# Halves of the pair's last unit two slots sooner and ahead of exponentials; the last eight sums of w_in one a step

## The chip, the cores and the metric

The kernel runs on one core of one Trainium2 chip. The metric is the device time of one execution in microseconds; the median of three runs is given. The core has TensorE (PE, matrix products), VectorE (DVE) and ScalarE (ACT) for elementwise work, GpSimd (POOL) and SyncE (SP), which here do hardly more than issue DMAs, and DMA engines that all queues share.

## The reference

Attention within chunks of 64 tokens, then an MLP with a leaky activation, then a bilinear MLP. All is float32; 2304 tokens, 512 features.

```python
# q, k, v: (4, 8, 576, 64); chunk 64
scores = scale * np.matmul(q_c, k_c.transpose(0, 1, 2, 4, 3))
attn = np.exp(scores - np.max(scores, axis=-1, keepdims=True))
attn = attn / (np.sum(attn, axis=-1, keepdims=True) + 1e-09)
out = np.matmul(attn, v_c)
x = out.transpose(0, 2, 1, 3).reshape(2304, 512)   # after the chunks are joined
h = x @ w_in                                       # 512 x 2048
x = (np.maximum(h, 0.0) + alpha * np.minimum(h, 0.0)) @ w_out
return (x @ w_a) * (x @ w_b) @ w2_out              # 512 x 1536, 1536 x 512
```

## The kernel before

Tokens are cut into 18 units of 128 (u = 0 to 17) and five blocks of 512, 256, 512, 512 and 512 tokens, so that units 10 to 17 make up the last two blocks, which the kernel calls the pair. Float32 operands are split into a high and a low half, and a product is three matmuls (`three`, L396): the names end in h and l. The weights of the first MLP lie in SBUF as such halves (`wi0h`, `wi0l` and so on).

The third block is the stretch of the change, some 184 to 291 us of the profile. It runs the first MLP of units 6 to 9 in 16 steps j. A step multiplies x by w_in (`psh`, 12 matmuls), `prelu` takes it through ACT (`neg` L414, `pos` L415), DVE (`pos` L416), ACT (`gh` L87) and DVE (`gl` L92), and one step later the result is multiplied by w_out into the accumulators (`acc`, 12 matmuls). Each step has two slots, 2j ahead of `prelu` and 2j+1 behind the matmuls of w_out (`advance`). Into these slots `att_line` puts the attention of the pair, by a table `at` of slots, one number for each unit. Steps are sorted by slot, and within a slot they stand in the order in which the list was put together. Engines run their instructions in program order, so this order is the order on every engine and queue.

For a unit of the pair the steps are these:

- `load_kq` (L245, issued by POOL): k and q into a buffer `kq`.
- `apart` (calls `halves`, L262 and L264): ACT copies k, then q, into the two 16-bit halves of each number (`kqd`, 128x1024 each), SP stores them to DRAM as `rowsk` and `rowsq`.
- `turn_qk` (calls `turned`, L269), two slots after `apart`: SP issues two DMA transposes that bring them back as `kT` and `qT`.
- `att_S` (L315) in `multiply`: 32 small products into `psSO`. Called S12 and so on here. In the same step the output product of the unit three before is made (`att_O`, L372), called O14 and so on. Its result goes through ACT (`xh`, or `x` for the last block) and DVE.
- `att_M` (DVE, L328 and L330), `soften` (exponential on ACT, L336, then the normalization on DVE, L341 to L345).
- the turn of e: by PE (`att_PT`) for units 10 to 13, by `halves` and a DMA transpose (`ed`, `rowse`, `eT`) for 14 to 17.

Unit 15's k and q are turned by PE instead (`att_kq`, `psT`, L298, with ACT copies `kT`, `qT`, L300). The PSUM pool of `psh`, `psSO`, `psT` and `psP` has four banks which go round.

The first eight sums of w_in (high half plus low half, DVE, L159) and their stores to DRAM (`wd`, POOL, L160) are made in an earlier block; the last eight in steps 8 to 11 of this one, two a step (`keep_w`). They are read back (`wir`) for the preparation of the second MLP. From slot 23 on, `y_sums` (L1248) and `begin_t` put DVE work for the second MLP into the same stretch; the last of these, `Txl` (L92), is needed by the first products of the second MLP (`psE`, L1348).

Of the kernel before, what the change touches and what calls it, by code (L numbers as in the profile page):

```python
# [18 lines left out]
def chunk_attention_prelu_mlp_bilinear_mlp(  # L19
# [17 lines left out]
    nc = tc.nc  # L37
# [9 lines left out]
    J1 = F1 // P  # L47
# [28 lines left out]
    def bank(nm="ps"):  # L76
        return ps_p.tile([P, DM], F32, tag="ps", name=nm)
# [5 lines left out]
    def wtile(name, dt=F32R):  # L83
        return wp.tile([P, DM], dt, tag="w", name=name)
# [67 lines left out]
    wparts = {}  # L152
    wd = [dr.tile([P, DM], F32, name=f"wd{j}") for j in range(J1)]

    def keep_w(j):

        hi, lo = W["i", j]
        x = wtile("wi", F32)
        nc.vector.tensor_tensor(out=x, in0=hi.bitcast(F32), in1=lo.bitcast(F32), op=ALU.add)  # L159
        nc.gpsimd.dma_start(out=wd[j], in_=x)  # L160

    def unpack_parts(i):
        u = unpack_ops(i, True)
# [86 lines left out]
    def load_v(u, queue=None):  # L250
        load("v", u, queue)
# [55 lines left out]
    def att_S(u, pss=None):  # L307
        qT, kT = att.pop(("qT", u)), att.pop(("kT", u))
        pss = pss or [att_bank(u, "psS") for _ in range(2)]
        for y in range(2):  # L310
            for c in range(2):
                for e in range(2):
                    for x in (e, 1 - e):
                        i = half(e), 2 * x + y, c
                        nc.tensor.matmul(  # L315
                            out=pss[e][half(x), half(2 * y + c)], lhsT=qT(*i), rhs=kT(*i),
                            start=True, stop=True,
                        )
        att["s", u] = pss
# [45 lines left out]
    def att_O(u, xh, xl, col, pss=None):  # L365
        eT, v_ = att.pop(("eT", u)), att.pop(("v", u))
        pss = pss or [att_bank(u, "psO") for _ in range(2)]
        for g in range(KD):
            x, y = divmod(g, 2)
            for c in range(2):  # L370
                for e in (c, 1 - c):
                    nc.tensor.matmul(  # L372
                        out=pss[c][half(e), half(g)], lhsT=v_[half(c), half(2 * g + e)],
                        rhs=eT[half(c), half(4 * e + 2 * y + x)], start=True, stop=True,
                    )
        cols = [slice(col + c * CH, col + (c + 1) * CH) for c in range(2)]
        return [
            (xh[:, :, f], None if xl is None else xl[:, :, f], ps[:, :KD * CH].rearrange("p (g i) -> p g i", g=KD))
            for f, ps in zip(cols, pss)
        ]  # L380
# [688 lines left out]
    def att_line(bx, x, ut, sums_of):  # L1069

        t0, n = blocks[bx]
        us = range(t0 // P, NU)
        LAG = 3

        def dest(u):
            if u * P < t0 + n:
                return *x, u * P - t0
            ut[u] = wtile(f"x{u}", F32).rearrange("p (k t) -> p k t", k=KD)
            return ut[u], None, 0

        def out_of(u, pss):
            o = att_O(u, *dest(u), pss)
            if u + 2 < NU:
                load_v(u + 2, nc.gpsimd)
            return o

        def multiply(w):
            pss = [bank("psSO") for _ in range(2)]
            now, then_ = us[w:w + 1], us[max(w - LAG, 0):max(w - LAG + 1, 0)]
            for u in now:  # L1090
                att_S(u, [ps[:, :KD * CH] for ps in pss])
            o = sum((out_of(u, [ps[:, KD * CH:] for ps in pss]) for u in then_), [])
            each(to_hi, o)

            def after():
                for u in now:
                    att_M(u)
                each(to_lo, o)

            return after  # L1100

        def soften(u):
            att_X(u)
            return lambda: weave(att_N(u))

        def out_only(*ws):
            pss = [bank("psSO") for _ in range(2)]
            o = sum((out_of(us[w], [ps[:, i * KD * CH:(i + 1) * KD * CH] for ps in pss])
                     for i, w in enumerate(ws)), [])
            each(to_hi, o)  # L1110
            return lambda: each(to_lo, o)

        def only(fn, *a):
            def step():
                fn(*a)
                return lambda: None

            return step

        at = {  # L1120
            "S": (0, 3, 6, 10, 13, 16, 19, 22), "turn": (5, 8, 11, 14), "out": (17, 19, 21, 25),
            "apart": (None, None, 1, 5, 7, None, 13, 17), "load": (None, None, None, 1, 4, 7, 10, 13),
        }
        steps = [(slot, lambda w=w: multiply(w)) for w, slot in enumerate(at["S"])]
        steps += [(slot + 1, lambda u=u: soften(u)) for u, slot in zip(us, at["S"])]
        steps += [(slot, only(att_PT, u, True)) for u, slot in zip(us, at["turn"])]
        steps += [(slot + 2, only(att_PT_in, u)) for u, slot in zip(us[KD:], at["out"])]
        steps += [(slot + 2, only(turn_qk, u)) for u, slot in zip(us, at["apart"]) if slot]
        steps += [(slot, only(att_PT_out, u)) for u, slot in zip(us[KD:], at["out"])]
        steps += [(13, only(att_kq, us[5]))]  # L1130
        steps += [(slot, only(apart, u)) for u, slot in zip(us, at["apart"]) if slot]
        steps += [(slot, only(load_kq, u, True, nc.gpsimd)) for u, slot in zip(us, at["load"]) if slot]
        steps += [(slot, lambda w=w: out_only(w)) for w, slot in ((5, 24), (6, 26), (7, 29))]
        steps += [(slot, only(fn)) for slot, fn in sums_of]
        return sorted(steps, key=lambda s: s[0])

    with tc.manual_schedule():
# [13 lines left out]
        x = xtiles("x")  # L1151
# [46 lines left out]
        bx, by = pairs[1]  # L1198
# [70 lines left out]
        for b, (t0, n) in enumerate(blocks[:bx]):  # L1269
            nxt = xtiles("x")  # L1270
            if b + 1 < bx:
                steps = att_steps(b + 1, nxt)
            else:
                XP["x"] = nxt
                for nm_, k0 in (("11", 0), ("12", 2)):
                    XP[nm_] = [tuple(t[:, k0 + kk, :] for t in nxt) for kk in range(2)]
                first_t = {}

                def begin_t():
                    sums_, first_t["split"] = t_steps(0)  # L1280
                    TX[0] = [(wtile("txh"), wtile("txl"))]
                    for _, fn in sums_ + first_t["split"].pop(0):
                        fn()

                steps = att_line(bx, nxt, ut, (
                    (20, lambda: load_raw(0)), (29, begin_t),
                    (23, lambda: y_sums(0)), (25, lambda: y_sums(1)), (27, lambda: y_sums(2)), (31, lambda: y_sums(3)),
                ))

            def advance(slot, steps=steps):  # L1290
                rest = []
                while steps and steps[0][0] <= slot:
                    rest.append(steps.pop(0)[1]())
                return rest

            def settle(rest):
                for then in rest:
                    then()

            for j in range(J1):  # L1300
                if b == 0:
                    if j in (1, 3):
                        load_qk(n0 + j // 2)
                    if j in (4, 6):
                        load_v(n0 + j // 2 - 2)
                h = h0[0][:, :n] if not (b or j) else s1(j, x, n)
                if b == 0:
                    g = prelu_unpacking(j, h, lambda: w_dma(min(2 * j + 9, NU1)), lambda: advance(2 * j), settle)
                else:
                    rest = advance(2 * j)  # L1310
                    g = prelu(j, h)
                    settle(rest)

                def second(b=b, j=j, g=g, n=n):
                    if j == 0:
                        acc[0] = new_acc()
                    s2(j, g, acc[0], n)
                    if j == J1 - 1:
                        end1(b, acc[0], n)

                pend.append(second)
                flush(2)
                settle(advance(2 * j + 1))
                if b == 1 and j % 2 == 1:
                    keep_w(j // 2)
                if b == bx - 1 and 0 <= j - J1 // 2 < J1 // 4:
                    for i in range(2):
                        keep_w(2 * j - J1 // 2 + i)
            x = nxt

        before_mlp2()
# [213 lines left out]
        for p, j in seq:  # L1545
# [8 lines left out]
            if not left[j] and j + 2 < J2:  # L1554
# [5 lines left out]
                i = units.index(("b", j + 2)) + 1  # L1560
# [89 lines left out]
```

## Time and profile before

| | |
|---|---|
| median of 3 runs | 867.23 us (866.1 to 867.29) |
| profiled execution | 864.8 us, span 863.0 us |
| PE busy | 841.9 us, 98% of the span |
| DVE busy | 658.6 us, 76% |
| ACT busy | 407.2 us, 47% |
| POOL busy | 25.2 us, 3% |
| chain that ended last | PE 83%, DVE 8%, DMA 4%, ACT 3% |
| DMA | 134.14 MB, mean 155 GB/s |

The span is the time between the first and the last instruction of the profiled execution; 1.8 us of its time lie around it. Busy shares are averages over stages with different limits. What a moved instruction is worth is read from the waits and the timelines of the stage in which it stands.

### The profile page before, as it was taken

To read this page: it belongs to the slowest core of one execution; us is meant where nothing else is said; L and a number is where in the kernel's file an instruction comes from. 1 tells how busy PE (TensorE), PEld (TensorE's weight loads), DVE (VectorE), ACT (ScalarE), POOL (GpSimd) and SP (SyncE) were. 2 spreads that over 40 slices of the span, in tenths; PEclk is the share of its full clock that TensorE was granted. 3 is DMA by queue.
4 is the path that set the end of the run, shared out by engine and by line. 5 is a ranking of instruction groups with operands and counts; after the bars stand their busy time and mean duration, and the time that the engine had idled before them with its cause. 6 is when DMAs were issued, how large, how long until landed. Compare 5 with 4: busy or idle time off the path is not lost.

```text
span 863.0 us, 14541 instructions
## 1 busy us (share of the span) xinstructions
PE 841.9 (98%) x5454; PEld 719.6 (83%) x5454; DVE 658.6 (76%) x1269; ACT 407.2 (47%) x777; POOL 25.2 (3%) x41
## 2 busy tenths in 40 slices
PE   7899999999989999999999999999999999999998
PEld 6778889987867788888888888888888888889998
DVE  5999975655558796867977898898898858848781
ACT  4677775545556554444754333333232325634440
POOL 0000000122120000000000000000000000000000
PEclk9999999999999999999999999999999999999999
DMA  9697679679394221232840354364364248925421
GB/s 218 168 254 216 196 171 233 163 173 190 87 218 113 99 98 49 74 118 77 301 139 31 128 203 140 134 232 141 134 231 141 86 143 299 301 75 185 138 72 49
DMA packets 144472, 134.14 MB, mean 155 GB/s; under 512 B 75793, under 2 KB 112145, under 8 KB 144401
## 3 DMA queue, kind: packets, MB, share of 16 engines
q1 hardware_dynamic: 141792, 124.82, 48.5%
q0 software_dynamic: 2608, 8.39, 3.7%
q8 instruction: 43, 0.70, 0.4%
q14 instruction: 29, 0.23, 0.1%
HBM read 82.32 MB, written 44.04 MB: 146 GB/s over the span
## 4 chain that ended last, share of the span: by engine, by line
PE 83%; DVE 8%; DMA 4%; ACT 3%; issue 1%; SPq 0%; DVEq 0%
PE acc L396 24%; PE psh L396 9%; PE psA L614 7%; PE psB L614 7%; PE psD L614 7%; PE psE L614 4%; PE psr L396 3%; PE psD L758 3%; PE psB L758 3%; PE psA L758 3%; PE psB L1348 3%; PE psD L1348 3%; PE psA L1348 2%; DMA qT<-rowsq 2%; PE psE L758 2%; PE psE L1348 1%
## 5 line engine op out<-in xcount | busy, mean ns | idle before, releaser
L416 DVE SCALAR_TENSOR_TENSOR pos<-neg,nalpha_sb,pos 128x512 f32<-128x512 f32 (+1 forms) x48 | 31.5, 657 | 36.6 <-ACT pos L415 36.5
L148 DVE SCALAR_TENSOR_TENSOR wx<-wx,wz 128x512 int32<-128x512 int32 x68 | 46.7, 687 | 13.5 <-ACT wx L136 11.6
L92 DVE TENSOR_TENSOR gl<-pos,gh 128x512 fp32r<-128x512 f32 (+1 forms) x56 | 34.4, 615 | 21.8 <-ACT gh L87 21.1
L87 ACT ACTIVATE gh<-pos 128x512 fp32r<-128x512 f32 (+1 forms) x56 | 32.0, 572 | 39.6 <-DVE pos L416 33.1
L644 DVE TENSOR_TENSOR t<-p,psB 128x512 f32<-128x512 f32 x48 | 32.8, 684 | 21.2 <-PE psB L614 16.9
L648 ACT ACTIVATE p<-psA 128x512 f32<-128x512 f32 x24 | 14.4, 598 | 71.8 <-PE psA L614 71.7
L136 ACT ACTIVATE wx<-raw 128x512 f32<-128x512 f32 x68 | 42.7, 669 | 1.1 <-DMA raw<-in_moe_w_out_dram 0.9
L654 ACT ACTIVATE p<-psD 128x512 f32<-128x512 f32 x24 | 14.4, 599 | 50.9 <-PE psD L614 42.4
L140 DVE TENSOR_SCALAR wz<-raw 128x512 uint16<-128x512 uint16 x68 | 31.2, 459 | 0.4 <-DMA raw<-in_moe_w_out_dram 0.4
L145 DVE TENSOR_SCALAR wz<-raw 128x512 uint16<-128x512 uint16 x68 | 30.8, 452 | 0.0
L682 ACT ACTIVATE b_sb<-psr 128x256 f32<-128x256 f32 x12 | 4.6, 384 | 52.5 <-PE psr L396 52.2
L414 ACT ACTIVATE neg<-psh 128x512 f32<-128x512 f32 (+1 forms) x48 | 24.8, 516 | 5.2 <-PE psh L396 5.2
L396 PE MATMUL psr<-xrh,Tl 128*128 128x256 f32 x96 | 27.2, 283 | 0.0
L396 PE MATMUL psr<-xrl,Th 128*128 128x256 f32 x96 | 27.2, 283 | 0.0
L396 PE MATMUL psr<-xrh,Th 128*128 128x256 f32 x96 | 27.1, 282 | 0.0
L1362 DVE SCALAR_TENSOR_TENSOR pos<-neg,beta_sb,psA 128x512 f32<-128x512 f32 x8 | 6.0, 747 | 26.4 <-ACT neg L1358 26.4
L415 ACT ACTIVATE pos<-psh 128x512 f32<-128x512 f32 (+1 forms) x48 | 25.2, 524 | 0.0
L262 ACT ACTIVATE kqd<-kq 128x1024 uint16<-128x1024 uint16 x22 | 22.1, 1050 | 0.7 <-DMA kq<-in_k_dram 0.4
L1358 ACT ACTIVATE neg<-p 128x512 f32<-128x512 f32 x24 | 15.2, 633 | 9.1 <-DVE p L1391 8.4
L336 ACT ACTIVATE e<-e 128x512 f32<-128x512 f32 x18 | 11.3, 629 | 16.6 <-DVE e L330 16.6
L396 PEld LDWEIGHTS psr<-xrh,Th 128*128 128x128 f32 x96 | 18.4, 192 | 0.4
L396 PEld LDWEIGHTS psr<-xrl,Th 128*128 128x128 f32 x96 | 18.4, 192 | 0.4
(950 smaller groups left out, 2997.9 us busy)
## 6 DMA issues: line engine op xcount, KB each, us to landing
raw<-in_moe_w_out_dram SPq DMA_DIRECT2D x28, 512.0 KB, 3.6
raw<-in_moe_w_in_dram SPq DMA_DIRECT2D x16, 512.0 KB, 5.3
raw<-in_moe_w_a_dram SPq DMA_DIRECT2D x12, 512.0 KB, 5.1
raw<-in_moe_w_b_dram SPq DMA_DIRECT2D x12, 512.0 KB, 4.8
cd<-t SPq DMA_DIRECT2D x24, 256.0 KB, 2.3
cd<-p SPq DMA_DIRECT2D x24, 256.0 KB, 2.0
wd<-wi POOLq DMA_DIRECT2D x16, 256.0 KB, 4.2
wir<-wd SPq DMA_DIRECT2D x16, 256.0 KB, 3.7
```

Source lines behind the costliest of these rows:

```text
L87: nc.scalar.activation(out=hi, in_=src, func=AF.Copy)
L92: nc.vector.tensor_tensor(out=lo, in0=src, in1=hi.bitcast(F32), op=ALU.subtract)
L136: return nc.scalar.activation(out=x.bitcast(F32), in_=hw.bitcast(F32), func=AF.Copy, scale=2.0 ** -112)
L140: yield nc.vector.tensor_scalar(out=z2[:, :, 0], in0=h2[:, :, 1], scalar1=13, scalar2=None, op0=ALU.logical_shift_right)
L145: yield nc.vector.tensor_scalar(out=z2[:, :, 1], in0=h2[:, :, 3], scalar1=1 << 15, scalar2=None, op0=ALU.bitwise_and)
L148: yield nc.vector.scalar_tensor_tensor(out=x, in0=x, scalar=3, in1=z, op0=ALU.logical_shift_left, op1=ALU.bitwise_or)
L396: nc.tensor.matmul(out=ps, lhsT=a, rhs=b, start=(i == 0 and first), stop=(i == n_i - 1 and a is wl))
L416: yield nc.vector.scalar_tensor_tensor(out=pos, in0=neg, scalar=nalpha_sb[:, j:j + 1], in1=pos, op0=ALU.mult, op1=ALU.add)
L614: nc.tensor.matmul(out=ps, lhsT=a, rhs=b, start=(start and kk == 0 and i == 0), stop=(kk == 1 and i == 2), skip_group_check=not start,)
L644: nc.vector.tensor_tensor(out=out, in0=a, in1=b, op=op)
L758: nc.tensor.matmul(out=ps[:, s * HALF:(s + 1) * HALF], lhsT=a, rhs=x[:, e], start=(start and s == 0 and i == 0 and n == 0), stop=(i == J2 ...
L1348: nc.tensor.matmul(out=ps, lhsT=a, rhs=b_, start=(start and kk == 0 and i == 0), stop=(kk == 1 and i == 2), skip_group_check=not start,)
```

## The change

Three things are changed. In `at`, the halves of unit 17 move from slot 17 to slot 15, and with them their transposes, which follow two slots later, from 19 to 17. In the list of steps, all `apart` steps move ahead of the `soften` and `turn_qk` steps, so that in a shared slot the halves come first. And `keep_w` is split into the sum (`keep_sum`) and the store (`keep_out`): in the third block sums 8 to 15 are made one a step in steps 8 to 15, and their stores are issued two a step from step 11 on.

```diff
--- before.py
+++ after.py
@@ -152,12 +152,19 @@
     wparts = {}
     wd = [dr.tile([P, DM], F32, name=f"wd{j}") for j in range(J1)]
 
-    def keep_w(j):
+    whole = []
+
+    def keep_sum(j):
 
         hi, lo = W["i", j]
         x = wtile("wi", F32)
         nc.vector.tensor_tensor(out=x, in0=hi.bitcast(F32), in1=lo.bitcast(F32), op=ALU.add)
-        nc.gpsimd.dma_start(out=wd[j], in_=x)
+        whole.append((j, x))
+
+    def keep_out(n):
+        for _ in range(min(n, len(whole))):
+            j, x = whole.pop(0)
+            nc.gpsimd.dma_start(out=wd[j], in_=x)
 
     def unpack_parts(i):
         u = unpack_ops(i, True)
@@ -1119,16 +1126,16 @@
 
         at = {
             "S": (0, 3, 6, 10, 13, 16, 19, 22), "turn": (5, 8, 11, 14), "out": (17, 19, 21, 25),
-            "apart": (None, None, 1, 5, 7, None, 13, 17), "load": (None, None, None, 1, 4, 7, 10, 13),
+            "apart": (None, None, 1, 5, 7, None, 13, 15), "load": (None, None, None, 1, 4, 7, 10, 13),
         }
         steps = [(slot, lambda w=w: multiply(w)) for w, slot in enumerate(at["S"])]
+        steps += [(slot, only(apart, u)) for u, slot in zip(us, at["apart"]) if slot]
         steps += [(slot + 1, lambda u=u: soften(u)) for u, slot in zip(us, at["S"])]
         steps += [(slot, only(att_PT, u, True)) for u, slot in zip(us, at["turn"])]
         steps += [(slot + 2, only(att_PT_in, u)) for u, slot in zip(us[KD:], at["out"])]
         steps += [(slot + 2, only(turn_qk, u)) for u, slot in zip(us, at["apart"]) if slot]
         steps += [(slot, only(att_PT_out, u)) for u, slot in zip(us[KD:], at["out"])]
         steps += [(13, only(att_kq, us[5]))]
-        steps += [(slot, only(apart, u)) for u, slot in zip(us, at["apart"]) if slot]
         steps += [(slot, only(load_kq, u, True, nc.gpsimd)) for u, slot in zip(us, at["load"]) if slot]
         steps += [(slot, lambda w=w: out_only(w)) for w, slot in ((5, 24), (6, 26), (7, 29))]
         steps += [(slot, only(fn)) for slot, fn in sums_of]
@@ -1322,10 +1329,11 @@
                 flush(2)
                 settle(advance(2 * j + 1))
                 if b == 1 and j % 2 == 1:
-                    keep_w(j // 2)
-                if b == bx - 1 and 0 <= j - J1 // 2 < J1 // 4:
-                    for i in range(2):
-                        keep_w(2 * j - J1 // 2 + i)
+                    keep_sum(j // 2)
+                    keep_out(1)
+                if b == bx - 1 and j >= J1 // 2:
+                    keep_sum(j)
+                    keep_out(2 * (j > 10))
             x = nxt
 
         before_mlp2()
```

On SP, in steps 3 to 5 of the third block, the names carry the unit (`rowsk13` is the store of unit 13's k, `kT13` its transpose). Before:

```order
L264 DMA rowsk13_2776<-kqd_2774 128x1024
L264 DMA rowsq13_2779<-kqd_2774 128x1024
L269 DMA_TRANSPOSE kT13_2841<-rowsk13_2776 128x4x256
L269 DMA_TRANSPOSE qT13_2843<-rowsq13_2779 128x4x256
L264 DMA rowsk14_2847<-kqd_2845 128x1024
L264 DMA rowsq14_2850<-kqd_2845 128x1024
L269 DMA_TRANSPOSE kT14_2902<-rowsk14_2847 128x4x256
L269 DMA_TRANSPOSE qT14_2904<-rowsq14_2850 128x4x256
```

Here the two transposes of unit 13 stand behind its own stores.

On SP, the same place in the changed kernel:

```order
L271 DMA rowsk13_2769<-kqd_2767 128x1024
L271 DMA rowsq13_2772<-kqd_2767 128x1024
L271 DMA rowsk14_2842<-kqd_2840 128x1024
L271 DMA rowsq14_2845<-kqd_2840 128x1024
L276 DMA_TRANSPOSE kT13_2848<-rowsk13_2769 128x4x256
L276 DMA_TRANSPOSE qT13_2850<-rowsq13_2772 128x4x256
L276 DMA_TRANSPOSE kT14_2902<-rowsk14_2842 128x4x256
L276 DMA_TRANSPOSE qT14_2904<-rowsq14_2845 128x4x256
```

The two stores of unit 14 stand ahead of the two transposes of unit 13.

On SP, in steps 7 to 9, before (`rowse14`, `eT14`: the exponentials of unit 14):

```order
L264 DMA rowsk16_3093<-kqd_3091 128x1024
L264 DMA rowsq16_3096<-kqd_3091 128x1024
L269 DMA_TRANSPOSE kT16_3158<-rowsk16_3093 128x4x256
L269 DMA_TRANSPOSE qT16_3160<-rowsq16_3096 128x4x256
L264 DMA rowse14_3246<-ed14_3244 128x1024
L264 DMA rowsk17_3250<-kqd_3248 128x1024
L264 DMA rowsq17_3253<-kqd_3248 128x1024
L269 DMA_TRANSPOSE eT14_3339<-rowse14_3246 128x4x256
L269 DMA_TRANSPOSE kT17_3341<-rowsk17_3250 128x4x256
L269 DMA_TRANSPOSE qT17_3343<-rowsq17_3253 128x4x256
```

Here unit 17's stores and transposes stand behind those of e14.

On SP, the same place in the changed kernel:

```order
L271 DMA rowsk16_3079<-kqd_3077 128x1024
L271 DMA rowsq16_3082<-kqd_3077 128x1024
L271 DMA rowsk17_3160<-kqd_3158 128x1024
L271 DMA rowsq17_3163<-kqd_3158 128x1024
L276 DMA_TRANSPOSE kT16_3165<-rowsk16_3079 128x4x256
L276 DMA_TRANSPOSE qT16_3167<-rowsq16_3082 128x4x256
L276 DMA_TRANSPOSE kT17_3251<-rowsk17_3160 128x4x256
L276 DMA_TRANSPOSE qT17_3253<-rowsq17_3163 128x4x256
L271 DMA rowse14_3257<-ed14_3255 128x1024
L276 DMA_TRANSPOSE eT14_3339<-rowse14_3257 128x4x256
```

The stores and transposes of unit 17 stand ahead of the store of e14, and the stores of unit 17 ahead of the transposes of unit 16.

On ACT, in step 6 (`kT15`, `qT15` are the copies of unit 15 out of PSUM; `kq16` is the input of unit 16's halves), before:

```order
L87 ACTIVATE xh_2568<-psSO_3038 128x4x64
L87 ACTIVATE xh_2568<-psSO_3039 128x4x64
L300 ACTIVATE kT15_3082<-psT_3077 128x512
L300 ACTIVATE qT15_3089<-psT_3084 128x512
L262 ACTIVATE kqd_3091<-kq16_2957 128x1024 x2
L336 ACTIVATE e14_3101<-e14_3101 128x512
```

Here the copies kT15 and qT15 stand right behind xh.

On ACT, the same place in the changed kernel:

```order
L87 ACTIVATE xh_2568<-psSO_3038 128x4x64
L87 ACTIVATE xh_2568<-psSO_3039 128x4x64
L269 ACTIVATE kqd_3077<-kq16_2957 128x1024 x2
L307 ACTIVATE kT15_3089<-psT_3084 128x512
L307 ACTIVATE qT15_3096<-psT_3091 128x512
L343 ACTIVATE e14_3101<-e14_3101 128x512
```

The halves of unit 16 stand ahead of the two copies. On ACT the halves of units 12 and 14 also move ahead of the exponentials e10 and e12, those of unit 13 ahead of the copy eT10, and those of unit 17 from behind `ed14` to behind the `gh` of step 7. On POOL the loads v15 and v16 go ahead of the first stores of these sums.

## Rows read from the trace of the kernel before

**Rows 1.** The page: the chain of work that ended last, by engine.
```profile
PE 83%; DVE 8%; DMA 4%; ACT 3%; issue 1%; SPq 0%; DVEq 0%
```

**Rows 2.** The waits from 176 to 296: engine, line, releaser; us in total, times, longest.
```profile
PE psSO L315 <- DMA qT<-rowsq: 6.2, 2, 4.1
```

**Rows 3.** Timeline of PE: start, length, instruction, [idle before, releaser].
```profile
196.27 0.69 PE L315 MATMUL psSO<-kT,qT 64*64 64x64 f32 x32 [2.07 <-DMA qT<-rowsq]
...
208.50 0.69 PE L315 MATMUL psSO<-kT,qT 64*64 64x64 f32 x32
...
220.91 0.50 PE L396 MATMUL psh<-xh,wi7h 128*128 128x512 f32 x1 [0.25 <-ACT kT L300]
...
252.98 1.14 PE L315 MATMUL psSO<-kT,qT 64*64 64x64 f32 x30 [4.13 <-DMA qT<-rowsq]
255.01 0.79 PE L396 MATMUL acc<-gh,wo9h 128*128 128x512 f32 x1
256.73 0.39 PE L396 MATMUL acc<-gl,wo9h 128*128 128x512 f32 x1
```

**Rows 4.** Timeline of SP's queue: start and length of issues in the third block.
```profile
199.16 1.25 SPq L269 DMA_TRANSPOSE qT<-rowsq  x1
...
202.88 0.33 SPq L264 DMA_DIRECT2D rowsq<-kqd  x1
...
244.74 4.60 SPq L269 DMA_TRANSPOSE qT<-rowsq  x1
```

**Rows 5.** The chain that ended last: start, length, what (170 to 310).
```profile
244.74 8.11 DMA qT<-rowsq
...
256.61 0.76 DVE pos L416
...
265.93 1.20 DVE wi L159 x2
```

**Rows 6.** Landing of DMAs, one answer per tile: five qT; qT13; rowsq14; eT14.
```profile
DMA to landing us min/median/max: 3.4/5.0/8.1
...
DMA to landing us min/median/max: 7.5/7.5/7.5
...
DMA to landing us min/median/max: 7.8/7.8/7.8
...
DMA to landing us min/median/max: 9.7/9.7/9.7
```

**Rows 7.** Timeline of ACT in the third block.
```profile
182.71 0.63 ACT L336 ACTIVATE e<-e 128x512 f32<-128x512 f32 x1 [2.08 <-DVE e L330]
...
209.69 0.66 ACT L87 ACTIVATE xh<-psSO 128x256 fp32r<-128x256 f32 x2 [3.55 <-PE psSO L372]
...
220.26 0.60 ACT L300 ACTIVATE kT<-psT 128x512 f32<-128x512 f32 x1
...
237.68 1.99 ACT L262 ACTIVATE kqd<-kq 128x1024 uint16<-128x1024 uint16 x2
...
249.91 1.06 ACT L262 ACTIVATE ed<-e 128x1024 uint16<-128x1024 uint16 x1 [2.58 <-DVE e L345]
254.94 0.66 ACT L87 ACTIVATE x<-psSO 128x256 f32<-128x256 f32 x2 [3.97 <-PE psSO L372]
```

**Rows 8.** Timeline of DVE in the third block.
```profile
186.23 0.75 DVE L416 SCALAR_TENSOR_TENSOR pos<-neg,nalpha_sb,pos 128x512 f32<-128x512 f32 x1 [1.01 <-ACT pos L415]
...
273.86 0.75 DVE L416 SCALAR_TENSOR_TENSOR pos<-neg,nalpha_sb,pos 128x512 f32<-128x512 f32 x1 [0.60 <-ACT pos L415]
...
290.41 1.28 DVE L92 TENSOR_TENSOR Txl<-wit,Txh 128x512 fp32r<-128x512 f32 x2
```

**Rows 9.** Windows: busy us of each engine, PE's granted clock, DMA share, GB/s.
```profile
232.00:234.00 2.00, 2.00 (x10) 1.64 (x9) 0.75 (x1) 1.18 (x3) 0.00 (x0) 1.00 0.00 0
254.00:256.00 2.00, 2.00 (x41) 1.72 (x34) 0.00 (x0) 1.06 (x4) 0.00 (x0) 0.50 0.98 326
260.00:270.00 10.00, 10.00 (x102) 7.85 (x101) 9.17 (x26) 6.23 (x19) 1.99 (x3) 1.00 0.31 92
```

## The prediction

> **What bounds the kernel now.** I read the page first: TensorE (PE) carries 83% of the chain of work that ended last, VectorE (DVE) 8% and DMA 4% [rows 1]. A change can therefore help only where PE stands still, or where the chain leaves PE. Next come the waits of the third block's stretch: one wait of PE is large, the score product `psSO<-kT,qT` on the transpose of q, 6.2 us in two pieces, the longer 4.1 [rows 2]. The timeline of PE finds them. The first is at 196.27, the scores of unit 12 (S12), 2.07 us; the second at 252.98, the scores of unit 17 (S17), 4.13 us [rows 3]. The same timeline shows scores that did not wait: S13, at 208.50, has no idle time ahead of it [rows 3].
>
> What is behind the second wait is seen in SyncE's (SP's) timeline: qT17 is issued only at 244.74, behind the turn of e14, and the chain shows it landing 8.11 us later, at 252.85 [rows 4, 5]. PE reads it 0.13 later. In the meantime the DMA engines are busy, while at 232 to 234 they carried nothing at all [rows 9]. Behind the stall PE runs for a while at the lower of its two clock levels (mean granted clock 0.50 at 254 to 256) [rows 9]. From there on the chain leaves PE for DVE (it goes through `pos` at 256.61, and the two sums of w_in at 265.93 lie on it) [rows 5]; DVE is busy 9.17 of 10 us there [rows 9].
>
> **The change part by part.** All shifts are against the profiled execution of 864.8 us (span 863.0). The median of the runs is 867.23, that is 2.43 more; I add the sum to the median.
>
> *S17.* The halves of unit 17's k and q come two slots sooner, and their two transposes stand behind those of unit 16 and no longer behind the store of e14 and eT14. Before, ScalarE (ACT) starts these halves at 237.68 [rows 7]; now they start right behind the `gh` some 10 us sooner, and by the issue spacing I estimate (from the 237.68 to 244.74 that the same steps took) that qT17 is issued near 235 and is there some 8 us ahead of its use, even at the slowest landing of the stretch, 9.7 [rows 6]. The stall goes whole: S17 would start at 252.98 − 4.13 = 248.85, where PE begins to wait [rows 3]. The output of unit 14 then follows at the full clock: `x` on ACT starts 254.94 − 252.98 = 1.96 after S17, while `xh` starts 209.69 − 208.50 = 1.19 after S13 [rows 3, 7]; another 0.77. Together **−4.9** for the moment at which DVE's stretch begins. ed15 on ACT would be in the way, ending at 249.91 + 1.06 = 250.97 against x at 248.85 + 1.19 = 250.04 [rows 7]; but it waits for DVE, which loses the 2 us ACT copy and two sums ahead of it, so it ends at about 249.5 and costs nothing. If this cover failed, the price is 0.9. The four MLP matmuls behind S17 that run slow (255.01 to 256.73, 1.72 us [rows 3]) give PE some more, which PE can't use, since DVE sets the pace there.
>
> *kT15.* The halves of unit 16 now stand ahead of ACT's copies kT15 and qT15 out of PSUM. The next product psh<-xh,wi7h takes over the PSUM bank and already waits for kT15's copy (0.25 idle at 220.91) [rows 3]. kT15 at 220.26 moves back by a pair of halves, 1.99 [rows 7]. All of it is on PE: **+1.99**. Nothing is there to hide it, as PE waits already.
>
> *S12.* The halves of unit 12 move ahead of the exponential e10, in front of which ACT stands idle for 2.08; a pair of halves takes 1.99 (as unit 17's at 237.68) [rows 7], so it fits. `neg` and `pos` of that step come 2 us sooner, but DVE waits only 1.01 for them [rows 8]. DVE's `xs`, the x2d stores that wait for it on SP, and kT12 and qT12 queued behind those stores all gain 1.0, and S12's stall of 2.07 becomes about 1.07: **−1.0**.
>
> *S13.* This is the open term. The halves of unit 14 move ahead of e12 into the same kind of idle time, and on SP their two stores (512 KB) now go ahead of kT13 and qT13. Before, qT13 was issued at 199.16 and took 7.5, so it landed at 206.7, and S13 at 208.50 did not wait [rows 3, 4, 6]. With S12's gain S13 is due at 207.5 and needs qT13 at 207.4. In the new order I estimate, by the spacing of the old issues, the stores at 198.3 and 199.2, kT13 at 199.6 and qT13 at about 201.0: 1.8 later. GpSimd's (POOL's) loads of kq15, v12, kq16 and v13 lie in the same stretch, and since they wait for the buffers which these halves empty, they go 1.5 to 2.7 sooner. How long does qT13 now take? The lower bound is the quickest of the five qT transposes, 3.4, and their middle, 5.0 [rows 6]: it lands at 204.4 to 206.0, no stall. At its own old 7.5 it lands at 208.5, stall 1.1. At eT14's 9.7 it lands at 210.7, stall 3.3. A second way: before, the pair that was second on SP's queue was rowsk14 and rowsq14, and rowsq14 was there at 202.88 + 7.8 = 210.7 [rows 4, 6]; now T13 is second, issued 1.9 sooner, so 208.8 to 210.7. I take 210.0, near the upper ends, because POOL's loads crowd in earlier than before. Stall: 210.0 + 0.13 − 207.5 = **+2.6**. I keep 0 and 4.6 (a landing at 212) as ends.
>
> The Trainium skill, page "DMA: Bandwidth & Descriptors", section "Latency and other measured facts", gives a DMA transpose 261 GB/s; by that 256 KB would be an estimated 1.0 us, T13 would be there long before S13, and the sum would come out by the first rival below. The rows of this stretch speak against it: the quickest of five took 3.4 from issue to landing [rows 6].
>
> *w_in's sums.* Before, wi8 to wi13 are summed by step 10 and wi14, wi15 at step 11, where a pair costs 1.20 on the chain [rows 5]. Now five (wi11 to wi15) lie in steps 11 to 15: three more where DVE sets the pace, at 0.60 each, 1.81. One gap takes one in: 0.60 idle ahead of `pos` at 273.86 [rows 8]; a sum doesn't fit into DVE's waits for `gh`, by its place in the order. So **+1.2** at `Txl` (290.41 [rows 8]), which PE's psE of the second MLP waits for. Bounds: 0 (PE has other work) and 1.8 (the gap closes).
>
> *POOL's stores.* v15 and v16 now go ahead of the stores of w_in, which come later and two a step. They are read back only in MLP2; the loads v15 to v17 go sooner. I cost it at nothing; the cover is the stretch from the last store (behind step 15) to its reading, and a store that lands late would show as a wait of `wir`'s readers, 0 to 1 us. The transposes eT14 to eT17 have fewer DMAs in front of them than before. T16 has more, the 512 KB of unit 17; but the DMA engines are idle there [rows 9], so nothing.
>
> **Sum:** −4.9 + 2.0 − 1.0 + 1.2 = −2.7 without S13; with +2.6 it is **−0.1**. 867.2 − 0.1 gives **867.1**.
>
> **The rivals.**
> First, T13 is in time (landing before 207.4): the sum stays −2.7, **864.5**. For it: half of the q transposes landed within 3.4 to 5.0 [rows 6]. Against it: its own old 7.5 already misses.
> Second, slower: T13 lands at 212 and the stall of 4.6 is as long as S17's was, so the clock falls as it did there: S and output lose 0.77 and the four matmuls about as much again (1.72 [rows 3], an estimated half of it lost at half the clock). Sum −2.7 + 4.6 + 1.6 = +3.5, **870.7**. It decides from about a landing at 210.5 (with the drop) or 212 (without): S12's 2.07 stall shows no such slow matmuls, S17's 4.13 does. For it: 512 KB ahead on SP's queue.
> In the Trainium skill, same page, section "Queues, rings and completion order", an engine takes packets from the rings in turn; by it POOL's loads and SP's queue share the engines, and a transpose behind two stores waits for both, which goes with the second rival. The trace agrees in so far as rowsq14 took 7.8 in that crowd [rows 6].
> Third, the S17 stall doesn't vanish, because qT17's tile is released late or unit 17's load (kq17) is: nearly all of the gain of 4.9 is lost, **871** to 872. Against it: the new place is some 10 us ahead.
>
> **How the numbers follow.** No difference (stall at S13 of 1.1 to 4.5 with the clock held, 865.5 to 869.0): 0.43. T13 in time or nearly: 0.29. T13 later with the clock fallen: 0.21. S17 still stalls: 0.07. A measurement of this kernel can tell about 0.2%, 1.7 us, from no change. So faster 0.29, same 0.43, slower 0.28. The range runs from the first rival with half of the sums' cost hidden, 864.0, to the second, 870.7.
>
> **What would show it.** Right: S17 without a wait; a wait of 2.2 for kT15 ahead of psh wi7; S12 waiting about 1.1; S13 waiting 1 to 4 for qT13; psE waiting more for Txl. The largest risk is qT13's landing: under 3 us of stall at the full clock is my case. The prediction is wrong if S17 still waits, if kT15's delay doesn't reach PE, or if S13's stall lies outside 1.1 to 4.5.

## The result, and the profile after

The changed kernel takes 879.33 us (878.16 to 880.7) where the kernel before takes 866.66 (864.88 to 867.29): a ratio of 1.015, with a 95% interval of 1.0127 to 1.0173, so 12.7 us slower. 867.1 was forecast, with a range of 864.0 to 870.7. The two profiled executions are 15.9 us apart (spans 878.9 and 863.0), because the one of before is at the low end of its runs and the one of after at the high end; the steps below add up to that difference.

The page of the changed kernel, the chain that ended last, by engine (before: [rows 1]):

```profile
PE 81%; DVE 9%; DMA 6%; ACT 2%; issue 2%; SPq 1%; DVEq 0%; ACTq 0%
```

DMA rises from 4% to 6% of the chain, which is where to look. The waits of PE from 176 to 296 (columns as in [rows 2]):

```profile
PE psSO L322 <- DMA qT<-rowsq: 18.1, 2, 16.8
...
PE psh L403 <- ACT kT L307: 2.1, 1, 2.1
```

The wait for q's transposes has grown from 6.2 to 18.1 us, and one piece of it is 16.8. The timeline of PE says which (before: [rows 3]; the lines of this kernel are 7 or 8 higher, so L322 is `att_S`, L403 the MLP matmul and L1356 the product `psE`):

```profile
194.81 0.70 PE L322 MATMUL psSO<-kT,qT 64*64 64x64 f32 x32 [1.36 <-DMA qT<-rowsq]
...
223.90 1.13 PE L322 MATMUL psSO<-kT,qT 64*64 64x64 f32 x32 [16.78 <-DMA qT<-rowsq]
225.81 0.79 PE L403 MATMUL acc<-gh,wo3h 128*128 128x512 f32 x1
...
236.38 0.69 PE L322 MATMUL psSO<-kT,qT 64*64 64x64 f32 x32
...
240.66 0.50 PE L403 MATMUL psh<-xh,wi7h 128*128 128x512 f32 x1 [2.10 <-ACT kT L307]
...
268.50 0.69 PE L322 MATMUL psSO<-kT,qT 64*64 64x64 f32 x32
...
306.97 0.50 PE L1356 MATMUL psE<-y22h,Txl 128*128 128x512 f32 x1 [0.71 <-DVE Txl L92]
```

and two rows of the kernel before which answer to it (S14 and the first product that needs `Txl`):

```profile
218.47 0.70 PE L315 MATMUL psSO<-kT,qT 64*64 64x64 f32 x32
...
291.15 0.50 PE L1348 MATMUL psE<-y22h,Txl 128*128 128x512 f32 x1
```

The piece of 16.78 is S13's, at 223.90. S17, at 268.50, has no wait any more. The distances between these stations say where the time went:

| stretch | before | after | difference |
|---|---|---|---|
| to the start of S12 | 196.27 | 194.81 | −1.46 |
| S12 to S13 | 12.23 | 29.09 | +16.86 |
| S13 to S14 | 9.97 | 12.48 | +2.51 |
| S14 to psh<-xh,wi7h | 2.44 | 4.28 | +1.84 |
| psh<-xh,wi7h to S17 | 32.07 | 27.84 | −4.23 |
| S17 to psE<-y22h,Txl | 38.17 | 38.47 | +0.30 |
| sum | | | +15.82 |

(0.46 of the first −1.46 stands already at S10, ahead of the first moved instruction.) S12 to S13, and S13 to S14 behind it, are where the loss lies; the other stretches come out near what was forecast. What happened to S13's operands is seen in SP's queue (before: [rows 4]) and in POOL's:

```profile
198.61 0.84 SPq L271 DMA_DIRECT2D rowsq<-kqd  x1
199.56 1.48 SPq L276 DMA_TRANSPOSE kT<-rowsk  x1
201.15 5.12 SPq L276 DMA_TRANSPOSE qT<-rowsq  x1
206.36 8.72 SPq L276 DMA_TRANSPOSE kT<-rowsk  x1
```

```profile
197.53 0.88 POOL L252 DMA_DIRECT2D kq<-in_k_dram  x1 [5.69 <-DVE gl L92]
200.15 0.88 POOL L252 DMA_DIRECT2D kq<-in_k_dram  x1
201.90 1.37 POOL L232 DMA_DIRECT2D v<-in_v_dram  x2
```

T13 (L276) is issued at 199.56 and 201.15. POOL has put kq15 (from 197.53) and v12 on its own queue before that, and kq16 (from 200.15) and v13 (201.90) come at the same time. The landings (us from issue to landing), one answer for each: kT13, qT13, the loads of kq16, and rowsq14, the last store ahead of T13 (before: [rows 6]):

```profile
DMA to landing us min/median/max: 18.4/18.4/18.4
...
DMA to landing us min/median/max: 22.6/22.6/22.6
...
DMA to landing us min/median/max: 17.4/19.4/21.4
...
DMA to landing us min/median/max: 5.0/5.0/5.0
```

T13 took 18.4 and 22.6 us where it took 4.8 and 7.5 before. The 512 KB of stores ahead of it are not slow: rowsq14 is there at 198.61 + 5.0 = 203.6. POOL's loads crawl as well, 17.4 to 21.4, and so does T14, which is issued right behind T13 (18.1 and 10.1). In windows (after the busy times: granted clock, DMA share, GB/s):

```profile
202.00:204.00 2.00, 2.00 (x10) 1.63 (x9) 0.71 (x1) 1.26 (x3) 1.27 (x2) 1.00 1.12 274
206.00:208.00 2.00, 1.11 (x5) 0.57 (x4) 0.00 (x0) 0.00 (x0) 0.00 (x0) 1.00 1.13 75
210.00:212.00 2.00, 0.00 (x0) 0.00 (x0) 0.00 (x0) 0.00 (x0) 0.00 (x0) 1.00 1.31 72
214.00:216.00 2.00, 0.00 (x0) 0.00 (x0) 0.00 (x0) 0.00 (x0) 0.00 (x0) 0.50 1.10 83
```

The DMA engines are fully busy (share 1.1 to 1.3), but they move 72 to 83 GB/s, where they moved 274 just before (62 to 92 over all windows of 2 us from 204 to 222). DVE, ACT and POOL stand idle in the last three windows, so it is no work of theirs that slows the transfers. And at 214 the granted clock of the idle PE is 0.50; S13, its output and the first MLP matmuls run at it (S13 1.13 long instead of 0.69), which is nearly all of the +2.51.

The same sign stood in the trace of the kernel before, twice, beside T13 itself and where T17 was late:

```profile
202.00:204.00 2.00, 2.00 (x12) 1.66 (x11) 0.81 (x2) 1.74 (x3) 0.85 (x1) 1.00 1.13 101
244.00:246.00 2.00, 2.00 (x11) 1.65 (x10) 2.00 (x6) 1.60 (x3) 0.31 (x1) 1.00 1.18 82
```

A full DMA share at 101 and 82 GB/s: at 202 with T13 and unit 14's stores on SP's queue and kq15, v12 and kq16 on POOL's, at 244 with eT14 and T17 on SP's and v15 and two pairs of w_in's stores on POOL's. I took that crowd for ordinary load, and T13's old landing of 7.5, which came from it, for a plain one.

### The profile page after: what moved, and what is told of

Read it like the earlier page. It is cut to its first block, busy times and chain, and to the rows that moved or that the text cites. A ratio compares the mean times of both kernels' runs of the same rounds, so it can differ in the third digit from the quotient of the medians.

```text
span 878.9 us, 14533 instructions
## 1 busy us (share of the span) xinstructions
PE 840.0 (96%) x5454; PEld 718.0 (82%) x5454; DVE 658.4 (75%) x1269; ACT 407.3 (46%) x777; POOL 25.1 (3%) x41
## 4 chain that ended last, share of the span: by engine, by line
PE 81%; DVE 9%; DMA 6%; ACT 2%; issue 2%; SPq 1%; DVEq 0%; ACTq 0%
PE acc L403 22%; PE psh L403 8%; PE psA L621 7%; PE psD L621 7%; PE psB L621 7%; PE psE L621 4%; PE psr L403 3%; DMA qT<-rowsq 3%; PE psD L765 3%; PE psB L765 3%; PE psA L765 3%; PE psB L1356 3%; PE psD L1356 2%; PE psA L1356 2%; PE psE L765 1%
## 5 line engine op out<-in xcount | busy, mean ns | idle before, releaser
L148 DVE SCALAR_TENSOR_TENSOR wx<-wx,wz 128x512 int32<-128x512 int32 x68 | 46.8, 688 | 13.5 <-ACT wx L136 11.6
L651 DVE TENSOR_TENSOR t<-p,psB 128x512 f32<-128x512 f32 x48 | 32.9, 684 | 21.2 <-PE psB L621 16.9
L322 PE MATMUL psSO<-kT,qT 64*64 64x64 f32 x448 | 9.9, 231 | 18.1 <-DMA qT<-rowsq 18.1
L403 PE MATMUL psr<-xrl,Th 128*128 128x256 f32 x96 | 27.2, 283 | 0.0
L403 PE MATMUL psr<-xrh,Tl 128*128 128x256 f32 x96 | 27.2, 283 | 0.0
L403 PE MATMUL psr<-xrh,Th 128*128 128x256 f32 x96 | 27.1, 283 | 0.0
L322 PEld LDWEIGHTS psSO<-kT,qT 64*64 64x64 f32 x448 | 8.2, 140 | 21.7 <-issue 20.0
L87 ACT ACTIVATE xh<-psSO 128x256 fp32r<-128x256 f32 x20 | 6.4, 380 | 27.1 <-PE psSO L379 27.1
```

What stands on the lines that cost most here:

```text
L87: nc.scalar.activation(out=hi, in_=src, func=AF.Copy)
L148: yield nc.vector.scalar_tensor_tensor(out=x, in0=x, scalar=3, in1=z, op0=ALU.logical_shift_left, op1=ALU.bitwise_or)
L403: nc.tensor.matmul(out=ps, lhsT=a, rhs=b, start=(i == 0 and first), stop=(i == n_i - 1 and a is wl))
L651: nc.vector.tensor_tensor(out=out, in0=a, in1=b, op=op)
```

## The experiments

Theory A: DMA transposes on SP's queue and transfers of POOL's queue that are in flight together slow each other several fold. In the changed kernel two things bring T13 into this: it is issued later, behind unit 14's stores, and the loads of kq16 and v13 come sooner, since unit 14's halves free their buffer sooner. Theory B: T13 is late because of the 512 KB that stand ahead of it on its own queue. Theory C: the place of T17, behind T16, is what delays. The first four runs take the change apart.

**Only unit 17's halves sooner (e1_slot).**

```diff
-            "apart": (None, None, 1, 5, 7, None, 13, 17), ...
+            "apart": (None, None, 1, 5, 7, None, 13, 15), ...
```

> Only unit 17's halves move from slot 17 to 15; list order and sums as before. Theory A (a DMA transpose and POOL's loads in flight together slow each other several fold; in the changed kernel the halves of unit 14 free a buffer sooner and so let POOL's loads of kq16 and v13 run into T13): T13 and the loads are placed as before, so S13 does not wait; T17 is issued near 235 with the DMA engines idle, S17's wait of 4.1 us goes and about 4.9 us with it, 0.994 of before. Theory B (T13 is late because 512 KB of stores stand ahead of it on SP's queue): the same, T13 stands first. Theory C (the move of T17 behind T16 is what delays): slower than before.

860.39 us against 867.33, ratio 0.9921 (0.9892 to 0.995). S13, S17 and the product that needs `Txl`, on PE:

```profile
208.27 0.69 PE L315 MATMUL psSO<-kT,qT 64*64 64x64 f32 x32
...
248.56 0.69 PE L315 MATMUL psSO<-kT,qT 64*64 64x64 f32 x32
...
286.00 0.50 PE L1348 MATMUL psE<-y22h,Txl 128*128 128x512 f32 x1
```

No wait at S13 or S17; from S17 to psE it is 37.44 where it was 38.17, near the 0.77 of S17's slow clock. C falls: this part of the change is a gain.

**Only the order of the list (e2_list).**

```diff
         steps = [(slot, lambda w=w: multiply(w)) for w, slot in enumerate(at["S"])]
+        steps += [(slot, only(apart, u)) for u, slot in zip(us, at["apart"]) if slot]
         steps += [(slot + 1, lambda u=u: soften(u)) for u, slot in zip(us, at["S"])]
...
-        steps += [(slot, only(apart, u)) for u, slot in zip(us, at["apart"]) if slot]
```

> Only the halves' place in the list is changed (ahead of exponentials and of the transposes of the same slot); unit 17 stays in slot 17, sums as before. A and B both: S13 waits some 17 us for qT13 as in the changed kernel, with S17's wait still there: 15 to 19 us slower than before, 1.018 to 1.022. C: about as before, 1.000 to 1.002.

879.94 us, ratio 1.0142 (1.0105 to 1.0178). S13 and S17:

```profile
222.30 1.14 PE L315 MATMUL psSO<-kT,qT 64*64 64x64 f32 x32 [15.42 <-DMA qT<-rowsq]
...
269.61 1.14 PE L315 MATMUL psSO<-kT,qT 64*64 64x64 f32 x30 [2.30 <-DMA qT<-rowsq]
```

The loss is all here: S13 waits 15.42, and T13 lands in 13.5 and 21.4. The ratio falls short of the 1.018 to 1.022 that I expected: S13's wait is 15.42 and not some 17, and S17's 2.30 and no longer 4.13.

**Only the sums (e3_sums).** `keep_sum` and `keep_out` as in the changed kernel, `at` and the list as before.

> Only the sums of w_in one a step in steps 8 to 15, stores two a step from step 11. All theories: Txl some 1.2 us later for the three sums in DVE's stretch. A adds: the stores wd8 to wd11 no longer run beside eT14 and T17, so S17's wait of 4.1 us shrinks to 0 to 3 us; sum 0 to 3 us faster than before. B: S17's wait stays 4.1, sum 1.2 slower, 1.0014.

863.05 us, ratio 0.9952 (0.9935 to 0.9968); a gain of 4.3 us by the medians, larger than the 0 to 3 that I expected. The rows show 1.1 of it (psE at 290.03 against 291.15); the profiled execution of the kernel before is 2.5 below the median of its runs here.

```profile
250.79 0.69 PE L322 MATMUL psSO<-kT,qT 64*64 64x64 f32 x32
...
290.03 0.50 PE L1356 MATMUL psE<-y22h,Txl 128*128 128x512 f32 x1 [0.69 <-DVE Txl L92]
```

S17 does not wait (its wait was 4.13), though T17 is issued no sooner than before (245.09 and 246.43): with v15 gone ahead and only one store of w_in near, T17 lands in 3.8 and 3.4 us instead of 7.7 and 8.1. Theory A had asked for that, B for an unchanged wait. From S17 to psE it is 39.24, 1.8 more than in e1_slot, where S17 doesn't wait either; I put that down to the three sums, though the stores and v15 and v16 are moved with them.

**T13 ahead of unit 14's stores again (e4_turnfirst).** The changed kernel with one line moved:

```diff
         steps = [(slot, lambda w=w: multiply(w)) for w, slot in enumerate(at["S"])]
+        steps += [(slot + 2, only(turn_qk, u)) for u, slot in zip(us, at["apart"]) if slot]
         steps += [(slot, only(apart, u)) for u, slot in zip(us, at["apart"]) if slot]
...
-        steps += [(slot + 2, only(turn_qk, u)) for u, slot in zip(us, at["apart"]) if slot]
```

> The changed kernel, but within a slot the transposes stand ahead of the halves, so T13 is ahead of unit 14's stores on SP's queue again; the halves stay ahead of the exponentials, so POOL's loads stay as early as in the changed kernel. A: T13 is issued near 196.5, most of it is done before kq16 starts at 200; S13 waits 0 to 3 us. B: no wait at S13. Either: S17 doesn't wait, kT15 costs 2, the sums 1.2: about 2.7 us faster than before, 0.997; if T13 should run into kq15 and v12 instead (197.5 to 203), A gives a wait of 5 us or more and B none.

861.73 us, ratio 0.9941 (0.9919 to 0.9964), better than the 0.997 that I expected. T13 on SP's queue, then kq15 and kq16 on POOL's, then the landings of kT13, qT13 and the first load of kq16:

```profile
196.46 1.23 SPq L276 DMA_TRANSPOSE kT<-rowsk  x1
197.79 1.25 SPq L276 DMA_TRANSPOSE qT<-rowsq  x1
```

```profile
197.85 0.88 POOL L252 DMA_DIRECT2D kq<-in_k_dram  x1 [6.06 <-DVE mx L335]
200.47 0.88 POOL L252 DMA_DIRECT2D kq<-in_k_dram  x1
```

```profile
DMA to landing us min/median/max: 4.7/4.7/4.7
...
DMA to landing us min/median/max: 5.8/5.8/5.8
...
DMA to landing us min/median/max: 7.6/7.6/7.6
```

POOL's loads come as early as in the changed kernel, but T13 is issued before them, and these three land in 4.7 to 7.6. S13, at 207.31, has no wait. So early loads alone don't do the harm. T13 was in flight until 203.6, beside kq15 (from 197.85), v12 (199.60) and kq16: that is the case in which theory A asked for a wait of 5 us or more and B for none. A as it stands is too simple; something more, such as which of the two is on its way first, has to come in. The next two runs decide on B: they keep the stores ahead of T13 and take the loads away.

**The loads on SP's queue (e5_kq16_on_sp, e5b_all_on_sp).** The changed kernel, with the loads of kq16 and v13 issued by SP; in e5b those of kq15 and v12 too.

```diff
-            load_v(u + 2, nc.gpsimd)
+            load_v(u + 2, nc.sync if u == us[1] else nc.gpsimd)       # e5b: u in us[:2]
...
-        only(load_kq, u, True, nc.gpsimd)
+        only(load_kq, u, True, nc.sync if u == us[6] else nc.gpsimd)  # e5b: u in us[5:7]
```

> The changed kernel, but the loads of kq16 and v13 are issued by SP, behind T14 on the same queue, and no longer by POOL. Unit 14's stores stay ahead of T13 on SP's queue. Theory A (T13 crawls because POOL's loads are in flight beside it): beside T13 there are only the ends of kq15 and v12, T13 lands in 5 to 9 us instead of 18.4 and 22.6, S13 waits 0 to 4 us instead of 16.8. Theory B (T13 crawls or waits because of the 512 KB ahead of it on its own queue): landing and wait stay as in the changed kernel.

> The changed kernel, but the loads of kq15, v12, kq16 and v13 are all issued by SP, behind T13 or T14. No POOL load is left beside T13. Theory A: kT13 and qT13 land in 3.5 to 5.5 us, as T12 does in the kernel before; S13 does not wait, or under 1 us. Theory B: T13 stays at 18 to 23 us, S13 waits some 17 us.

863.28 and 863.15 us, one run each, beside 866.82 for the kernel before. kT13 and qT13 in e5:

```profile
DMA to landing us min/median/max: 7.3/7.3/7.3
...
DMA to landing us min/median/max: 6.4/6.4/6.4
```

and in e5b:

```profile
DMA to landing us min/median/max: 3.7/3.7/3.7
...
DMA to landing us min/median/max: 3.4/3.4/3.4
```

Unit 14's stores stand ahead of T13 as in the changed kernel, and T13 lands in 7.3 and 6.4, and with no POOL load beside it in 3.7 and 3.4. S13 waits 0.72 in e5 and not at all in e5b. B falls. Both runs also put the loads behind T13 in time (kq15 at 203.24 in e5b), so they don't tell POOL's queue from the order of arrival; the next two do.

**The cost by itself (g1_reload_pool, g2_reload_sp).** The kernel before with kq17 loaded a second time into its own buffer, in slot 14, by POOL or by SP, ahead of T16, where little else moves.

```diff
+        steps += [(14, only(again_kq, us[7], nc.gpsimd))]   # g2: nc.sync
```

> The kernel before, with one load added: POOL loads kq17 (512 KB) a second time, right behind the first, so that it is in flight when SP issues T16 at 225.7 and 228.2, where the kernel before has little else in flight and T16 lands in 3.2 and 3.4 us. Theory A: kT16 and qT16 take 8 us or more and the second load takes far over the 4 to 5 us of the first. Theory B: T16 stays at 3 to 5 us.

> The kernel before, with the same second load of kq17 issued by SP, directly ahead of T16 on its queue. Theory A: same bytes, but one queue, so nothing crawls: T16 lands in 3 to 6 us after its issue. Theory B: 512 KB ahead of T16 on its queue, so T16 takes as long as T13 in the changed kernel, 15 us or more.

868.01 and 866.68 us, one run each. Landings in g1 of kT16, qT16, the second half of the added load, and v15:

```profile
DMA to landing us min/median/max: 6.8/6.8/6.8
...
DMA to landing us min/median/max: 10.8/10.8/10.8
...
DMA to landing us min/median/max: 9.3/9.3/9.3
...
DMA to landing us min/median/max: 10.0/10.0/10.0
```

and kT16 and qT16 in g2:

```profile
DMA to landing us min/median/max: 5.0/5.0/5.0
...
DMA to landing us min/median/max: 4.4/4.4/4.4
```

From SP's queue the 512 KB cost kT16 1.8 us and qT16 1.0 (5.0 and 4.4 against 3.2 and 3.4); from POOL's they cost 3.6 and 7.4 (6.8 and 10.8), and the load's own second half slows down from 4 to 9.3. Not all of the 7.4 is the added load's: on POOL's queue it also pushes v15 (256 KB) back from 222.71 to 229.97, so qT16, issued at 229.17, runs beside the load's second half (256 KB), v15 and the end of the first half. Both are POOL's, so the queue is what differs between g1 and g2; theory A's prices are from one execution each. kT16, at 6.8, stayed under the 8 I had asked for.

**Towards a better kernel (h2_best, h4_sums_early).** h2 is e1_slot with unit 12's transposes one slot sooner, ahead of the x2d stores; h4 makes the sums three, three and two in steps 8 to 10 as well.

```diff
-        steps += [(slot + 2, only(turn_qk, u)) ...
+        steps += [(slot + 2 - (u == us[2]), only(turn_qk, u)) ...
```

```diff
-                if b == bx - 1 and 0 <= j - J1 // 2 < J1 // 4:
-                    for i in range(2):
-                        keep_w(2 * j - J1 // 2 + i)
+                if b == bx - 1 and 0 <= j - J1 // 2 < 3:
+                    for i in range(3 - (j - J1 // 2) // 2):
+                        keep_w(3 * j - J1 + i)
```

> Only unit 17's halves in slot 15 (as in e1_slot) and unit 12's transposes one slot sooner, so that they stand ahead of the x2d stores on SP's queue. Theory A: with no POOL load beside T12 it is issued near 187 and lands in 3.5 to 5.5 us, so S12's wait of 2.4 goes: 1.5 to 2.4 us faster than e1_slot, near 0.990 of before. Against it: x2d's stores behind T12 delay kT13's issue; S13 has some 2 us to spare.

> As h2_best, and the last eight sums of w_in three, three and two a step in steps 8 to 10, so that none is left in the stretch in which DVE sets the pace. If a sum costs 0.6 there, 1.2 us faster than h2_best, near 0.9885 of before. Theory A's risk: POOL's stores of the sums then run beside eT14 and eT15, which would make their output products wait.

858.05 us, ratio 0.9912 (0.9888 to 0.9935), and 857.28 us, 0.9896 (0.9876 to 0.9917), before at 867.0. S13, S17 and psE of h2, then of h4:

```profile
205.94 0.69 PE L315 MATMUL psSO<-kT,qT 64*64 64x64 f32 x32 [0.61 <-DMA qT<-rowsq]
...
246.21 0.69 PE L315 MATMUL psSO<-kT,qT 64*64 64x64 f32 x32
...
283.66 0.50 PE L1348 MATMUL psE<-y22h,Txl 128*128 128x512 f32 x1
```

```profile
205.15 0.69 PE L315 MATMUL psSO<-kT,qT 64*64 64x64 f32 x32
...
245.43 0.69 PE L315 MATMUL psSO<-kT,qT 64*64 64x64 f32 x32
...
282.85 0.50 PE L1348 MATMUL psE<-y22h,Txl 128*128 128x512 f32 x1
```

In h2 the wait at S12 is gone and psE comes 2.34 sooner than in e1_slot, as expected. h4 is not told apart from h2 by the intervals, and its reason fails: from S17 to psE it is 37.42, in h2 37.45. Two sums fewer in that stretch bring nothing; the 0.8 us between the two profiles is S13's wait of 0.61 and its surroundings. Both beat the kernel before and the changed one.

## Why the prediction was wrong

Of the six terms, four came out as forecast, POOL's stores were put at nothing, and S13, which I had marked as the open term, was off by 16.8 us.

- S17: −4.1 of wait was forecast and −4.2 came (psh<-xh,wi7h to S17). That T17 would be issued well ahead was right; so was ed15's staying out of the way (0.35 of idle time ahead of `x`).
- kT15: +1.99 forecast, 1.84 came; the wait is 2.10 where it was 0.25. Right.
- S12: −1.0 forecast, and −1.0 came behind S10. The size was right in part by luck: the wait itself fell by 0.71, to 1.36 and not to 1.07, and the rest came from shorter gaps of PE ahead of it, which I had not forecast.
- The tail: −0.77 + 1.2 = +0.4 forecast, +0.30 came. The size was right. The reason was right only in part: I said that DVE alone sets the pace behind S17, and h4 shows that with S17 on time taking sums away brings nothing. Adding them goes with 1.0 more in the changed kernel and 1.8 in e3_sums (against e1_slot), and psE then waits 0.7 for `Txl` from DVE.
- POOL's stores: nothing forecast. e3_sums shows that moving them, with v15 ahead of them, takes S17's wait away by itself. The changed kernel also moves T17, which does the same (e1_slot), so there the two can't be told apart.
- S13: +2.6 forecast, with ends of 0 and 4.6; +16.9 came, and another 2.5 from the lower clock behind it. The step that failed is the bound. I saw that T13 would be issued 1.8 later and that POOL's loads would come 1.5 to 2.7 sooner, and both happened (qT13 at 201.15 against 199.16, kq15 at 197.53 against 199.19, kq16 at 200.15 against 203.15). Then I bounded the landing by the slowest landing in the stretch, 9.7, and by the time at which the old second pair on SP's queue was through. Both assume that the DMA engines move bytes at the rate they moved them before. They didn't: the rate itself fell to 72 to 83 GB/s. The second rival named the place (T13 late, the clock fallen) but had it decide on the 512 KB ahead on SP's queue, at 4.6 us. e5b shows that these cost nothing by themselves (3.7 and 3.4 behind the same stores). The loads beside T13 do it, and by g1 and g2 it matters that they are on the other queue.

The sentence on rings in the Trainium skill ("DMA: Bandwidth & Descriptors", section "Queues, rings and completion order"), by which an engine takes packets from the rings in turn, agrees with both transfers being slow at once; from it one would expect each to get a share of the rate, and it does not say that the sum of both falls to under a third, as the windows shown have it. The 261 GB/s of a transpose in the Trainium skill (same page, "Latency and other measured facts") is not seen here as a time to landing: qT13 took 3.4 us in e5b and 22.6 in the changed kernel.

With 16.9 + 2.5 in S13's place, my sum −2.7 becomes +16.7, against 15.8 between the profiles. And where T13 is quick, the rest of the change is a gain, as the sum without S13 said: 5.6 us in e4_turnfirst by the medians, 3.5 and 3.7 in the single runs of e5 and e5b.

What stays open is why the crawl is so much worse in one overlap than in another. In e4 T13 and the loads of kq15 and kq16 overlap too, and qT13 lands in 5.8; it was issued first there. In g1 and in the changed kernel the loads were on their way first. But going first doesn't free a transpose: in e3_sums qT13 was issued at 199.70, just ahead of kq15 (199.71), and took 8.8, with kq16 at 9.3 to 10.0 and 57 GB/s at a share of 0.84 from 204 to 206. No run changed the order alone, or the amount in flight alone, and what in the DMA engines slows both is not shown.

## What to carry to other kernels

Before an edit moves a DMA, look at what will be in flight beside it, on every queue, and not only at what stands ahead of it on its own. A window in which the DMA share is full and the GB/s are low is a sign of transfers that slow each other, and an edit that lengthens this overlap is not bounded by the slowest landing seen so far. And a change of this kind is several changes: the line that paid (unit 17 two slots sooner, 0.9921) and the one that cost (the order of the list, 1.0142) were separate. The order of the list is itself two: e4_turnfirst keeps the halves ahead of the exponentials, gives up only their place ahead of the transposes, and with the rest of the change is at 0.9941.

## What was not expected of the hardware

- DMA transposes from SP's queue and loads from POOL's, in flight together, moved 72 to 83 GB/s at a DMA share of 1.1 to 1.3. A transpose of 256 KB that lands in 3.4 us with a quiet POOL queue (qT16 before, qT13 in e5b) took 10.8 beside some two loads of 256 KB from POOL (g1) and 22.6 beside v12, kq16 and v13, 1 MB, with T14 behind it (the changed kernel). 512 KB from SP's own queue, ahead of it, cost it 1.0 (g2).
- A PE wait of 16.8 us left the engine at the lower clock for its next matmuls: the granted clock was 0.50 from about 214 on, while PE was idle, and the stretch behind the wait took 2.51 longer. Short waits go either way: after one of 2.38 at S12 the granted clock stayed at 1.00 in e1_slot and fell to 0.50 in g1_reload_pool, and after one of 2.27 (S12 in e3_sums) and one of 2.30 (S17 in e2_list) it fell to 0.50 in the windows behind. My rival set S12's 2.07, without slow matmuls, against S17's 4.13; the length of the wait alone does not tell the two cases apart.
